# A Conformer layer: later weight loads and weight preparation, and a depthwise convolution shifted so that it no longer waits for the next group

## The chip, the cores and the metric

The kernel runs on one core of one Trainium2 chip. The metric is the device time of one execution in microseconds (us), lower is better.

Engines as the profile names them: PE is TensorE (matmuls and transposes), PEld its weight loads, DVE VectorE, ACT ScalarE, POOL GpSimd, SP SyncE, which issues most transfers ("SPq" is a transfer that it issues).

## The reference, cut to what matters

Two sequences (B = 2) of T = 4000 tokens with D = 512 features go through one Conformer layer in bfloat16.

```python
x1 = x  + 0.5 * silu(layernorm(x)  @ w_ff1_a) @ w_ff1_b          # FFN 1, 512 -> 2048 -> 512
h  = layernorm(x1);  q, k, v = h @ w_q, h @ w_k, h @ w_v
x2 = x1 + softmax(q @ k.T * scale) @ v @ w_o                     # attention over all 4000 tokens
h  = layernorm(x2) @ w_pw1;  h = h[..., :D] * sigmoid(h[..., D:])  # gate (GLU)
dc = depthwise_conv(h, dw)                                       # 15 taps along time, 7 to each side
dc = (dc - mean) / sqrt(var + 1e-5)                              # over both sequences: all of dc first
x3 = x2 + silu(dc) @ w_pw2
out = layernorm(x3 + 0.5 * silu(layernorm(x3) @ w_ff2_a) @ w_ff2_b)
```

## The kernel before

The kernel works on groups of 500 tokens: 8 groups (NG) per sequence, each of 4 tiles (TPG) of 125 tokens (P). Per sequence, phase A does FFN 1 and the projections of all groups. Phase B does attention, gate and convolution. After both sequences phase D does the rest. The weights w_q and w_k are multiplied together once at the start, and so are w_v and w_o (the "weight fusion").

The framework's scheduler fixes one static list of instructions per engine when the kernel is built. It orders them by a priority that counts up in program order, and by its own estimate of when things are ready. `tc.cur_priority` lets the program move a piece forward (a lower number) or back.

Attention of one tile takes four blocks of 1000 keys. Each block is a chain over three engines:

```python
def attention_tile(qg, x1g, x2g, i):
    for j in range(NBLK):                                    # 4 blocks
        sps = psum.tile(..., name="s_ps", tag="s")           # two buffers in all
        ...   8 matmuls: scores                              # PE   s_ps
        nc.vector.tensor_reduce(negm[:, j:j+1], sps, op=ALU.max, negate=True)   # DVE  negm
        nc.scalar.activation(pexp, sps, ACT.Exp, bias=negm[:, j:j+1], ...)      # ACT  pexp
        ...   8 transposes of pexp                           # PE   pt_ps
        nc.scalar.copy(pts, ptp)                             # ACT  pt_sb
        ...   8 matmuls with V                               # PE   o_ps
        nc.scalar.copy(obuf[:, j, :], ops)                   # ACT  obuf
    ...                                                      # DVE: weights of the blocks, x2g
```

The convolution of group g is cut into four blocks of 128 channels. Five taps of a block are matmuls with diagonal matrices on PE (`conv_ps`), ten are steps on DVE (`cacc`, the last one writes `dcg`). The DVE steps get a low priority, so that they fill gaps. A convolution needs 7 positions of its right neighbour, so group g is only scheduled when the gate of group g + 1 is done:

```python
def conv_c(g, c, dcg):
    for k in range(NPE): ...                    # 5 matmuls on PE
    saved = tc.cur_priority
    tc.cur_priority = saved + CONV_PRIO_OFFSET  # 3000: low
    for k in range(NPE, KW): ...                # 10 steps on DVE
    nc.vector.bn_stats(...)
    tc.cur_priority = saved

def glu_front(g, x2g):
    ...                                         # norm, transposes, gate
    if g > 0:
        ...                                     # POOL copies 7 positions each way
        schedule_conv(g - 1)
    if g == NG - 1:
        schedule_conv(g)

def schedule_conv(g):
    for c in range(KD):
        pending.append(lambda c=c: conv_c(g, c, dcg))
    pending.append(lambda: conv_fin(g, dcg))    # a fifth item: only one store
```

The work of gate and convolution is handed out between the attention tiles of the next group:

```python
for g in range(NG):
    ...
    for i in range(TPG):
        attention_tile(qg, x1g, x2g, i)
        for _ in range(-(-len(pending) // (TPG - i))):      # rounded up
            pending.popleft()()
    nc.sync.dma_start(tok_view(x2s, b, g), x2g[:])
    pending.appendleft(lambda g=g, x2g=x2g: glu_front(g, x2g))
while pending:
    pending.popleft()()
```

After the first tile the gate runs and adds five items. Then ceil(5/3) = 2, ceil(3/2) = 2 and 1 items follow after tiles two, three and four. So convolution blocks stand after the second and the third tile, two each, and after the fourth only the store.

## Time and profile before

The median was 2663.91 us (2661.47 to 2666.32 in four runs).

| before | |
|---|---|
| profiled span | 2659.7 us |
| PE, DVE, ACT busy | 89%, 60%, 45% |
| steady attention group (groups 3 to 6, which repeat alike) | 80.8 us |
| attention of a sequence, first to last store of x2s | 568.6 us and 571.9 us |
| tail: last store of x2s to the first load of the next phase | 75.0 us and 74.1 us |

From the page of the kernel before: the busy times, then the busy tenths of PE, the granted PE clock and the DMA share in 40 equal slices of 66 us, then the shares of the engines in the chain of work that ended last.

```profile
PE 2374.0 (89%) x12943; PEld 1383.0 (52%) x12944; DVE 1601.4 (60%) x3004; ACT 1190.7 (45%) x1866; POOL 94.1 (4%) x119
...
PE   6999989999999972699989999999997299999998
...
PEclk8999999999999995799999999999999599999999
DMA  4111110000000000211120000000002121111100
...
PE 71%; DVE 14%; ACT 9%; DMA 2%; issue 2%; SPq 1%; POOL 0%; ACTq 0%; POOLq 0%; DVEq 0%
```

PE is the bottleneck nearly everywhere, and the holes in its row (the seams) are the start, the change from sequence 1 to sequence 2, and the end of sequence 2's attention. There the clock falls as well.

The timeline of SP gives the rhythm of phase B, as one x2s store ends each group (columns: start, duration of the issue, engine, line, operation, output<-input, count).

```profile
665.27 0.27 SPq L426 DMA_DIRECT2D x2s<-x2g  x1
...
746.09 0.27 SPq L426 DMA_DIRECT2D x2s<-x2g  x1
...
987.35 0.26 SPq L426 DMA_DIRECT2D x2s<-x2g  x1
...
1062.36 0.38 SPq L109 DMA_DIRECT2D wa<-in_w_ff_a_dram  x1
...
1063.34 11.35 SPq L223 DMA_DIRECT2D xg<-in_x_dram  x2
```

A steady group takes 746.09 - 665.27 = 80.8 us. From the last group of sequence 1 (987.35) 75 us pass until the loads of sequence 2 are issued (1062.36), weights first, x behind them. The steady group as a window (columns: from and to, length, then the busy us of PE, PEld, DVE, ACT and POOL with their numbers of instructions, the PE clock, the DMA share, GB/s):

```profile
665.27:746.09 80.82, 77.66 (x456) 46.94 (x454) 67.85 (x115) 46.96 (x73) 1.83 (x3) 1.00 0.08 26
```

PE is recorded busy for 77.7 of 80.8 us; 3.2 us are idle.

### The profile page before, as it was taken

Reading aid. Unit: us, or ns where it says so; the run is one execution under the profiler, and the core shown is the slowest. Engines: PE = TensorE matmul, PEld = TensorE weight load, DVE = VectorE, ACT = ScalarE, POOL = GpSimd, SP = SyncE. Lnnn points to the kernel's source line nnn. Section 1 sums busy time; section 2 is a strip of 40 time slices with the busy share of each in tenths; the row PEclk is TensorE's granted clock in tenths of the full one; section 3 lists DMA queues with packets and bytes.
Section 4 is the critical chain, followed back from the end, with each engine's and each line's share of the span. In section 5 each row is a group of like instructions: output and inputs, shape, how many; then the busy total and the mean of one; then the engine's idle time right before and its main releaser. Section 6 shows DMA issues by size and latency. Waiting matters only on the chain.

```text
span 2659.7 us, 32574 instructions
## 1 busy us (share of the span) xinstructions
PE 2374.0 (89%) x12943; PEld 1383.0 (52%) x12944; DVE 1601.4 (60%) x3004; ACT 1190.7 (45%) x1866; POOL 94.1 (4%) x119
## 2 busy tenths in 40 slices
PE   6999989999999972699989999999997299999998
PEld 3555555555555540355545555555554055555554
DVE  3344345598888888344334558988888844444443
ACT  2433255555555540233426556555553143334432
POOL 0000000000000000000000000000000000000000
PEclk8999999999999995799999999999999599999999
DMA  4111110000000000211120000000002121111100
GB/s 119 47 46 33 47 39 24 24 32 13 20 32 32 17 16 17 97 39 43 39 70 16 16 24 32 32 14 19 32 16 87 54 63 47 47 47 47 39 25 23
DMA packets 77065, 101.32 MB, mean 38 GB/s; under 512 B 9456, under 2 KB 66160, under 8 KB 76912
## 3 DMA queue, kind: packets, MB, share of 16 engines
q1 hardware_dynamic: 76912, 99.24, 11.6%
q8 instruction: 101, 1.65, 0.3%
q14 instruction: 52, 0.43, 0.1%
HBM read 58.28 MB, written 40.96 MB: 37 GB/s over the span
## 4 chain that ended last, share of the span: by engine, by line
PE 71%; DVE 14%; ACT 9%; DMA 2%; issue 2%; SPq 1%; POOL 0%; ACTq 0%; POOLq 0%; DVEq 0%
PE ff_acc L200 17%; PE ff_ps L188 17%; PE o_ps L392 16%; PE s_ps L370 7%; DVE cacc L306 6%; ACT pt_sb L389 5%; PE pt_ps L387 3%; DVE negm L376 3%; PE q_ps L246 2%; PE pwb_ps L339 2%; PE pwa_ps L347 2%; PE pw_ps L470 2%; PE v_ps L258 2%; ACT pexp L380 2%; ACT obuf L395 1%
## 5 line engine op out<-in xcount | busy, mean ns | idle before, releaser
L370 PE MATMUL s_ps<-KT,qgB 128*125 128x500 bf16 x2048 | 506.0, 376 | 8.9 <-issue 4.6
L392 PE MATMUL o_ps<-V,pt_sb 125*125 125x512 bf16 x2048 | 486.8, 383 | 16.6 <-ACT pt_sb L389 4.5
L188 PE MATMUL ff_ps<-ln_hT,wa 128*128 128x500 bf16 x2048 | 444.2, 376 | 8.5 <-DVE ln_hT L179 8.4
L200 PE MATMUL ff_acc<-wb,ff_h 128*125 128x512 bf16 x2048 | 447.3, 379 | 0.0
L192 ACT ACTIVATE ff_h<-ff_ps 128x500 bf16<-128x500 f32 x512 | 300.3, 587 | 328.0 <-PE ff_ps L188 326.9
L376 DVE TENSOR_REDUCE negm<-s_ps 125x1 f32<-125x1000 f32 x256 | 306.0, 1196 | 207.2 <-PE s_ps L370 206.6
L380 ACT ACTIVATE pexp<-s_ps,negm 125x1000 bf16<-125x1000 f32 x256 | 280.0, 1094 | 262.3 <-DVE negm L376 184.5
L392 PEld LDWEIGHTS <-pt_sb 125*125 125x125 bf16 x2048 | 263.0, 136 | 229.4 <-ACT pt_sb L389 100.6
L200 PEld LDWEIGHTS <-ff_h 128*125 128x125 bf16 x2048 | 278.4, 137 | 160.3
L306 DVE SCALAR_TENSOR_TENSOR cacc<-gt,dwT,cacc 128x500 f32<-128x500 bf16 x512 | 355.0, 729 | 0.2
L370 PEld LDWEIGHTS <-qgB 128*125 128x125 bf16 x2048 | 260.3, 137 | 129.7 <-issue 12.8
L188 PEld LDWEIGHTS <-wa 128*128 128x128 bf16 x2048 | 199.4, 97 | 246.1 <-issue 18.1
L389 ACT COPY pt_sb<-pt_ps 125x1000 bf16<-125x1000 bf16 x256 | 251.8, 991 | 82.7 <-PE pt_ps L387 79.4
L395 ACT COPY obuf<-o_ps 125x512 f32<-125x512 f32 x256 | 149.1, 582 | 155.2 <-PE o_ps L392 155.0
L387 PEld LDWEIGHTS <-pexp 125*125 125x125 bf16 x2048 | 156.5, 137 | 116.1 <-ACT pexp L380 85.1
L387 PE MATMUL pt_ps<-ident,pexp 125*125 125x125 bf16 x2048 | 166.3, 222 | 54.6 <-ACT pexp L380 54.6
L181 ACT COPY ln_hT<-ln_tr 128x1000 bf16<-128x1000 bf16 x48 | 47.7, 993 | 323.0 <-PE ln_tr L176 323.0
L159 POOL TENSOR_TENSOR ln_rstd<-ln_ve,mhalf 125x4 f32<-125x4 f32 x80 | 86.8, 1089 | 2234.5 <-DVE ln_ve L157 2219.0
L176 PE MATMUL ln_tr<-ident,ln_hn 125*128 125x125 bf16 x1024 | 74.7, 227 | 92.3 <-DVE ln_hn L165 92.3
L473 DVE TENSOR_TENSOR x3g<-pw_ps,x2gD 125x512 bf16<-125x512 f32 x64 | 42.2, 679 | 182.2 <-PE pw_ps L470 182.2
L297 PE MATMUL conv_ps<-gt,diagw 128*128 128x500 bf16 x320 | 83.1, 403 | 44.2 <-DVE cacc L306 43.9
L176 PEld LDWEIGHTS <-ln_hn 125*128 125x128 bf16 x1024 | 65.3, 101 | 109.4 <-issue 51.7
(84 smaller groups left out, 1749.8 us busy)
## 6 DMA issues: line engine op xcount, KB each, us to landing
xg<-in_x_dram SPq DMA_DIRECT2D x16, 500.0 KB
x1s<-x1g SPq DMA_DIRECT2D x16, 500.0 KB
qts<-qg SPq DMA_DIRECT2D x16, 500.0 KB
qgB<-qts SPq DMA_DIRECT2D x16, 500.0 KB
x1gB<-x1s SPq DMA_DIRECT2D x16, 500.0 KB
x2s<-x2g SPq DMA_DIRECT2D x16, 500.0 KB
dcs<-dcg SPq DMA_DIRECT2D x16, 500.0 KB
dcgD<-dcs SPq DMA_DIRECT2D x16, 500.0 KB
```

Source lines behind the costliest of these rows:

```text
L176: nc.tensor.transpose(tr[:, kk, i, :P], hn[:, i, k * 128 : (k + 1) * 128], ident[:P, :P])
L188: nc.tensor.matmul(ps[:, :G], wa[:, k, f * 128 : (f + 1) * 128], hT[:, k, :], start=(k == 0), stop=(k == KD - 1))
L192: nc.scalar.activation(h1[:], ps[:, :G], ACT.Silu)
L200: nc.tensor.matmul(ps[:P, :D], h1s[f][:, i * P : (i + 1) * P], wb[:, f, :], start=(f == 0), stop=(f == KF - 1))
L306: nc.vector.scalar_tensor_tensor(o_ap, gt[:, c, k : k + G], dwT[:, c, k : k + 1], in1, op0=ALU.mult, op1=ALU.add)
L370: nc.tensor.matmul(sps[:P, c, :G], qg[:, k, i * P : (i + 1) * P], KT[:, k, j * KB + c * G : j * KB + (c + 1) * G], start=(k == 0), stop=(k ...
L376: nc.vector.tensor_reduce(negm[:, j : j + 1], sps[:P, :CPB, :G], axis=AX.XY, op=ALU.max, negate=True)
L380: nc.scalar.activation(pexp[:], sps[:P, :CPB, :G], ACT.Exp, bias=negm[:, j : j + 1], scale=1.0, accum_out=lsum[:, j : j + 1],)
L387: nc.tensor.transpose(ptp[:P, u, :P], pflat[:, u * P : (u + 1) * P], ident[:P, :P])
L389: nc.scalar.copy(pts[:], ptp[:P, :UPB, :P])
L392: nc.tensor.matmul(ops[:P, :D], pts[:, u, :], V[:, j * UPB + u, :], start=(u == 0), stop=(u == UPB - 1))
L395: nc.scalar.copy(obuf[:, j, :], ops[:P, :D])
```

## The change

The change wants to shorten the places where PE stands idle. It has two halves.

*Loads.* The first x tile is loaded before the FFN weights, and the first FFN weight in four chunks. The weight fusion moves behind the first half of the first FFN, its loads to ACT's queue.

*Convolution.* Output positions are shifted left by 7. The convolution of group g then needs only its own group and 14 positions of its left neighbour, and is scheduled by the gate of group g itself. One group instead of two is left after the last attention tile. Each block stores its own result, so the fifth pending item is gone.

```diff
-                wa = load_weight(wpool, w_ff1_a, "wa1")
-                wb = load_weight(wpool, w_ff1_b, "wb1")
+                wa = alloc_weight(wpool, w_ff1_a, "wa1")
+                wb = alloc_weight(wpool, w_ff1_b, "wb1")
 ...
                 xg_c, hT_c = a_front(0)
+                fill_weight(wa, w_ff1_a, col_chunks=4)
+                fill_weight(wb, w_ff1_b)
                 h1_c = ffn_a(h1pool, psum, hT_c, wa)
+                if b == 0:
+                    fused_weight_prep(wpool, psum)           # was: at the very start
 ...
-                def conv_c(g, c, dcg):
+                def conv_c(g, c, gt):
+                    o0 = PAD if g == 0 else 0
+                    o1 = G + PAD if g == NG - 1 else G
+                    W = o1 - o0
+                    pos0 = g * G - PAD + o0
 ...
+                    nc.sync.dma_start(dcs[b, :, c, pos0 : pos0 + W], dcc[:, :W])
                     tc.cur_priority = saved
-                def conv_fin(g, dcg):
-                    nc.sync.dma_start(dcs[ch], dcg[:])
 ...
-                    if g > 0:
-                        prev = gts[g - 1]
-                        nc.gpsimd.tensor_copy(gt[:, :, 0:PAD], prev[:, :, G : G + PAD])
-                        nc.gpsimd.tensor_copy(prev[:, :, PAD + G : PAD + G + PAD], gt[:, :, PAD : 2 * PAD])
-                        schedule_conv(g - 1)
-                    if g == NG - 1:
-                        schedule_conv(g)
+                    (before the gate) nc.gpsimd.tensor_copy(gt[:, :, 0:LH], prev_gt[0][:, :, G : G + LH])
+                    for c in range(KD):
+                        pending.append(lambda c=c: conv_c(g, c, gt))
```

("..." marks cuts. Phase D only follows the new layout of dcs and loads its first FFN weight in chunks.)

## The prediction

> **What bounds it now.** The page shows PE busy 2374 of 2660 us (89%); in the FFN stretches (1092 to 1359, 2150 to 2648) PE is busy over 98% at clock 1.00, so they cannot shrink. Steady attention groups (80.8 us apart by the stores of x2s) have PE busy 77.8 of 81, DVE 67.8. What is left are the seams, seen in the chain in order of time and the timeline:
> - Start: x is queued behind 6 MB of weights, first read at 31.3 us, although the weight fusion ended near 26; first FFN matmul 40.9.
> - End of attention, batch 0: last attention matmul at 983, last convolution on DVE at 1060, its store landed at 1062. DVE runs two groups' convolutions alone, 8 of one channel block each; one is 10 steps of about 0.65 us and a statistic of 0.6, 7.1 us; four are 28.4.
> - Start of batch 1: both FFN weights (4 MB) are issued at 1062.4 before x; x is read at 1080.4, first FFN matmul 1089.9.
> - Batch 1 has the same tail (2032 to 2111), then the last phase, whose weights are already there.
>
> **What the change does.**
> 1. Convolution g no longer waits for the right neighbour (output shifted 7 positions to the left), so one group instead of two is left after the last attention tile. The instruction order confirms: 40 steps of the last group plus 10 left over, against 84. In their place group 1 of each batch gets a convolution. Group 1 takes 83.1 us without any, group 2 82.6 with one, steady ones 80.8: I expect it to be free. Gain 28 us per batch, 56 in all; the 10 left-over steps fill DVE gaps (6 us) of the gate's matmuls.
> 2. Batch 1, x before weights: a 500 KB load alone landed in 3.4 us (dcgD at 2113). From there to the first FFN matmul took 9.5 us, of which 1.5 is a wait and 1.2 another tile's statistics; so 7. First FFN matmul 10.5 us after the issue instead of 27.5: gain 17. The first 512 KB chunk of weights lands sooner at the 250 GB/s of 1062 to 1080.
> 3. Start: x lands near 11 us (the tap loads ahead of it land at 9.8), the 20 diagonal builds (3.3 us) sit inside its normalization, FFN starts near 21. Then the weight fusion, some 12 us with its waits (wv and wo reuse the buffers of wq and wk, so load late); the second FFN matmul group starts near 49 instead of 56. Gain 7. Loads on the ACT queue gain little in themselves: the Trainium skill, "Trainium Kernel Development and Optimization", Key Constraints, says that queues share the same 16 DMA engines and only issue time is saved.
> 4. Added: 4 stores of 126 KB for one of 500 KB, 1000-byte rows in the last phase's loads. Both off the chain (DMA share 4 to 9% in attention).
>
> 1, 2 and 3 all lie on the chain, as PE is idle there. Sum 28+28+17+7 = 80. Prediction 2585 us, range 2562 to 2614; faster by over 2% 0.88, within 2% 0.11, slower 0.01.
>
> **What would show it.** Last attention matmul to last convolution 48 us instead of 77; x issue to FFN in batch 1 10 to 12 us; first FFN matmul at 19 to 24; attention groups still 80 to 83 us; PE busy time unchanged.
>
> **What would make it wrong.** The fourth convolution moves to the group's last tile, so its low-priority DVE steps may hold up the next group's maxima: 1 us per group costs 14. Group 1 may grow. The late wv/wo loads may stall PE at the start.

## The result, and the profile after

The changed kernel takes 2650.1 us (2645.96 to 2653.55, 9 runs), the kernel before 2662.47 us (13 runs). The ratio is 0.995, with a 95% interval of 0.9941 to 0.996: no difference by the 2% criterion, where 3% were predicted.

The same lines of the page, for the changed kernel:

```profile
PE 2377.3 (90%) x12942; PEld 1379.3 (52%) x12944; DVE 1612.6 (61%) x2998; ACT 1186.8 (45%) x1866; POOL 93.5 (4%) x105
...
PE   5999989989999994799989999999998399999998
...
PEclk9999999999999997899999999999999699999999
DMA  4110110100001000311020001000000411111100
...
PE 61%; DVE 26%; ACT 7%; issue 2%; DMA 2%; POOL 1%; SPq 0%; ACTq 0%; POOLq 0%; DVEq 0%
```

PE's work is the same (2377.3 for 2374.0 us). The holes at the ends of attention became smaller, as intended (their slices 7 2 became 9 4 in sequence 1 and 7 2 became 8 3 in sequence 2). Between the holes the slices are too coarse to show a loss, but DVE's share of the chain rose from 14% to 26%, with DVE's work up by only 11 us. The same places in the timeline of SP:

```profile
674.72 0.27 SPq L437 DMA_DIRECT2D x2s<-x2g  x1
...
759.58 0.27 SPq L437 DMA_DIRECT2D x2s<-x2g  x1
...
1014.87 0.27 SPq L437 DMA_DIRECT2D x2s<-x2g  x1
...
1062.09 0.29 SPq L236 DMA_DIRECT2D xg<-in_x_dram  x1
1062.42 6.05 SPq L116 DMA_DIRECT2D wa<-in_w_ff_a_dram  x4
```

The tail shrank from 75.0 to 1062.09 - 1014.87 = 47.2 us. But a steady group now takes 759.58 - 674.72 = 84.9 us for 80.8. In its window the work is the same to within 1.1 us on every engine:

```profile
674.72:759.58 84.86, 78.22 (x454) 46.61 (x453) 68.94 (x115) 46.65 (x73) 1.66 (x2) 1.00 0.08 25
```

PE's idle time in it is 84.86 - 78.22 = 6.6 us, for 3.2 before.

Laid out along the time axis, the two profiled spans differ by 11.2 us, which adds up so:

| stretch | predicted | measured, before minus after, us |
|---|---|---|
| start, to the first matmul of the second FFN half | 7 | 56.15 - 54.97 = 1.2 |
| attention of sequence 1 | 0 | 568.6 - 597.3 = -28.7 |
| tail of sequence 1 | 28 | 75.0 - 47.2 = 27.8 |
| sequence 2, loads issued to first FFN matmul | 17 | 27.5 - 15.5 = 12.0 |
| attention of sequence 2 | 0 | 571.9 - 595.7 = -23.8 |
| tail of sequence 2 | 28 | 74.1 - 49.7 = 24.4 |
| all else (rest of phase A, phase D) | 0 | -1.7 |
| sum | 80 | 11.2 |

The tails gave 52.2 us, and attention took 52.5 us back. That is the main question. The second is why start and second sequence gave 13 for 24.

Where does PE stand idle in a group, if the work is the same? The list of waits in the steady group (engine, line and tile that waited, what released it, then us in total, times, longest) names the transposes of the exponentials. Before:

```profile
ACT pexp L380 <- DVE negm L376: 9.8, 12, 1.5
...
PEld L387 <- ACT pexp L380: 3.2, 3, 1.7
...
PE pt_ps L387 <- ACT pexp L380: 2.1, 2, 1.3
```

After:

```profile
ACT pexp L389 <- DVE negm L385: 14.3, 11, 2.1
...
PEld L396 <- ACT pexp L389: 8.2, 7, 2.0
...
PE pt_ps L396 <- ACT pexp L389: 5.3, 4, 1.6
```

The transposes waited 5.3 us for the exponentials instead of 2.1 (their weight loads, which overlap PE, 8.2 instead of 3.2), in a group that grew by 4.0. One such place in the timeline of the changed kernel (a bracket is idle time before, and its releaser):

```profile
737.96 1.94 PE L401 MATMUL o_ps<-V,pt_sb 125*125 125x512 bf16 x8
...
739.73 2.06 PE L379 MATMUL s_ps<-KT,qgB 128*125 128x500 bf16 x9
...
740.14 0.74 DVE L421 SCALAR_TENSOR_TENSOR x2g<-obuf,cw,oacc 125x512 bf16<-125x512 f32 x1
740.80 2.29 DVE L385 TENSOR_REDUCE negm<-s_ps 125x1 f32<-125x1000 f32 x2
742.08 1.09 ACT L389 ACTIVATE pexp<-s_ps,negm 125x1000 bf16<-125x1000 f32 x1 [1.56 <-DVE negm L385]
...
743.19 1.09 ACT L389 ACTIVATE pexp<-s_ps,negm 125x1000 bf16<-125x1000 f32 x1
...
743.32 0.67 PE L396 MATMUL pt_ps<-ident,pexp 125*125 125x125 bf16 x8 [1.52 <-ACT pexp L389]
...
744.37 3.84 DVE L330 SCALAR_TENSOR_TENSOR cacc<-gt,dwT,cacc 128x500 f32<-128x500 bf16 x5
...
745.36 2.97 PE L401 MATMUL o_ps<-V,pt_sb 125*125 125x512 bf16 x13
```

PE does nine score matmuls in a row (739.73): by count and semaphores, the last one of a block and all eight of the next. What its list has next are the transposes of the first of these two blocks. Its maximum on DVE, its exponential on ACT and then its transposes follow one after the other, and PE stands 1.52 us. Part of that is DVE, which starts the maximum 0.7 us after the scores end, because it still has x2g to do; the rest is that eight matmuls are shorter than the detour. The output matmuls of an earlier block (737.96), which could have filled the gap, stand in the list before the last score matmul; those at 745.36 need these very transposes.

### The profile page after: what moved, and what is told of

It reads as the page before. It is cut to its first block, busy times and chain, and to the rows that moved or that the text cites. A ratio compares the mean times of both kernels' runs of the same rounds, so it can differ in the third digit from the quotient of the medians.

```text
span 2648.5 us, 32618 instructions
## 1 busy us (share of the span) xinstructions
PE 2377.3 (90%) x12942; PEld 1379.3 (52%) x12944; DVE 1612.6 (61%) x2998; ACT 1186.8 (45%) x1866; POOL 93.5 (4%) x105
## 4 chain that ended last, share of the span: by engine, by line
PE 61%; DVE 26%; ACT 7%; issue 2%; DMA 2%; POOL 1%; SPq 0%; ACTq 0%; POOLq 0%; DVEq 0%
PE ff_acc L213 17%; PE ff_ps L201 17%; PE o_ps L401 9%; DVE cacc L330 9%; DVE negm L385 6%; PE s_ps L379 5%; DVE oacc L421 3%; ACT pt_sb L398 3%; ACT pexp L389 3%; PE pt_ps L396 2%; PE q_ps L259 2%; PE pw_ps L487 2%; PE v_ps L271 2%; PE pwa_ps L361 1%; DVE x2g L421 1%
## 5 line engine op out<-in xcount | busy, mean ns | idle before, releaser
L330 DVE SCALAR_TENSOR_TENSOR cacc<-gt,dwT,cacc 128x500 f32<-128x500 bf16 (+2 forms) x512 | 362.7, 732 | 3.5
L398 ACT COPY pt_sb<-pt_ps 125x1000 bf16<-125x1000 bf16 x256 | 251.7, 990 | 86.5 <-PE pt_ps L396 85.0
L396 PE MATMUL pt_ps<-ident,pexp 125*125 125x125 bf16 x2048 | 167.8, 224 | 98.6 <-ACT pexp L389 97.9
L216 DVE SCALAR_TENSOR_TENSOR x1g<-ff_acc,xg 125x512 bf16<-125x512 f32 x64 | 44.0, 688 | 104.4 <-PE ff_acc L213 104.4
```

The costliest lines, as they stand in the source:

```text
L330: nc.vector.scalar_tensor_tensor(o_ap, gt[:, c, o0 + k : o0 + k + W], dwT[:, c, k : k + 1], in1, op0=ALU.mult, op1=ALU.add)
L396: nc.tensor.transpose(ptp[:P, u, :P], pflat[:, u * P : (u + 1) * P], ident[:P, :P])
L398: nc.scalar.copy(pts[:], ptp[:P, :UPB, :P])
```

## The experiments

All outputs are right. Steady group means a stretch between two neighbouring x2s stores in the middle of sequence 1.

### Is it the hand-out of the blocks? (e1, e2)

The change drops the fifth pending item. Four items over three tiles are handed out 2, 1, 1 instead of 2, 2, 1, so the fourth block moves behind the group's last tile. e1 gives the changed kernel an empty fifth item; e2 takes the fifth item from the kernel before.

```diff
 # e1, on the changed kernel
                     for c in range(KD):
                         pending.append(lambda c=c: conv_c(g, c, gt))
+                    pending.append(lambda: None)
 # e2, on the kernel before
-                    for c in range(KD):
+                    for c in range(KD - 1):
                         pending.append(lambda c=c: conv_c(g, c, dcg))
-                    pending.append(lambda: conv_fin(g, dcg))
+                    pending.append(lambda: (conv_c(g, KD - 1, dcg), conv_fin(g, dcg)))
```

> The changed kernel with one empty item put back on the pending list, after the four convolution blocks, so that the list has five items again and the rounding-up split hands out 2, 2, 1 per tile (blocks 0,1 in tile 1, blocks 2,3 in tile 2, nothing in tile 3) as in the kernel before, in place of 2, 1, 1. Nothing else differs. Theory A (the spread over the tiles cost the time, because the fourth block's steps now stand before the next group's maxima): steady attention groups go from 84.9 back to about 80.8 us, total about 2650 - 50 = 2600 us, ratio to before about 0.977. Rival B (a convolution one group earlier is not free, whatever its place in the group): groups stay at 84.9, total 2650, ratio 0.995. Rival C (the four small stores or the three-deep dcc ring hold up DVE or the queue): also stays at 84.9.

> The kernel before with its closing item (the store) folded into the fourth block's item, so that the list has four items and is handed out 2, 1, 1. Nothing of the change is in it. Theory A: its steady groups go from 80.8 to about 84.9 us in groups 2 to 7 of both batches, total about 2663 + 12 x 4 = 2710 us, ratio about 1.018. Rivals B and C: same time as before, ratio 1.00, groups 80.8.

e1 took 2603.5 us (ratio to before 0.9786, 0.9769 to 0.9802), its steady groups 80.8 us. e2 took 2706.24 us (1.0167, 1.0151 to 1.0182), its steady groups 84.9 us. So an item that does nothing gives 47 us back to the changed kernel, and the kernel before, with nothing of the change in it but four items for five, falls to the same 84.9. The hand-out is the cause. How it acts was still open.

### Four stores for one? (e3)

```diff
-                    dcc = work.tile([128, 512], BF16, name="dcc", tag="dcc", bufs=3)
+                    dcc = dcg[:, c, :]                 # one tile for the four blocks of a group
-                    nc.sync.dma_start(dcs[b, :, c, pos0 : pos0 + W], dcc[:, :W])
+                    if c == KD - 1:
+                        nc.sync.dma_start(dcs[b, :, :, pos0 : pos0 + W], dcg[:, :, 0:W])
```

> The changed kernel with one 500 KB store per group, issued after the fourth block, from a two-deep tile as in before, in place of four stores of 126 KB from a three-deep ring; still four items, 2, 1, 1. Theory A: no change, steady groups 84.9, total 2650 within 5 us. Rival C: groups back to about 81, total about 2600.

It took 2650.37 us with groups of 84.9. The stores cost nothing, and that rival falls.

### Why x came late in sequence 2 (e4)

In the changed kernel x stands first in the queue, yet DVE reads it 8.6 us after its issue (1070.70 - 1062.09, below), where the prediction took 3.4 us from another 500 KB load. One difference is that x is laid over 125 partitions, the other (dcgD) over 128 (dcgD also comes in longer rows; e4 tests the partitions). The Trainium skill, "DMA: Bandwidth & Descriptors", section "Why a DMA increments its semaphore by 16 and not by 1", says that a transfer runs on the largest number of engines up to 16 that divides the size of the slowest dimension on both its sides; by that rule 125 gives 5, 120 gives 15. e4 loads the first x tile of each sequence as 120 + 5 partitions.

```diff
-                    nc.sync.dma_start(xg[:], tok_view(x, b, g))
+                    if g == 0:
+                        xv = tok_view(x, b, g)
+                        nc.sync.dma_start(xg[0:120], xv[0:120])
+                        nc.sync.dma_start(xg[120:P], xv[120:P])
+                    else:
+                        nc.sync.dma_start(xg[:], tok_view(x, b, g))
```

> The changed kernel with the first x tile of each batch loaded as 120 + 5 partitions in place of 125. In the profile of after the first x tile of batch 1 took 8.5 us from issue to first use though nothing was queued ahead of it, with a DMA share of 0.31, that is 5 of 16 engines; 125 has the divisor 5 and 120 the divisor 15. Theory D (few engines carry the tile): issue to first use about 4 us, first FFN matmul of batch 1 about 11 us after the issue instead of 15.5, total 4 to 8 us below the changed kernel. Rival E (the weights issued behind x take its bandwidth): issue to first use stays at 8 us, total unchanged.

The windows just after the issue in sequence 2 (the last two columns are the mean DMA share of 16 engines and GB/s, the column before them the PE clock), first of the changed kernel, then of e4:

```profile
1062.00:1066.00 4.00, 0.00 (x0) 0.00 (x0) 0.00 (x0) 0.00 (x0) 0.00 (x0) 0.50 0.31 89
```

```profile
1056.30:1060.90 4.60, 0.00 (x0) 0.00 (x0) 0.00 (x0) 0.00 (x0) 0.00 (x0) 0.50 0.80 186
```

A share of 0.31 is 5 of 16 engines, and 89 GB/s over 4 us are 356 KB, less than the 512 KB of x, although the weights were being issued behind it from 1062.42 on. With the split the share is 0.80 (the weights behind x included, as 186 GB/s over 4.6 us are more than x). DVE reads x 4.6 us after its issue instead of 8.6. The first reads of x on DVE, first in the changed kernel (issue at 1062.09), then in e4 (issue at 1056.30):

```profile
1070.70 1.29 DVE L167 BATCH_NORM_STATS2 ln_st<-xg 125x6 f32<-125x512 bf16 x2 [9.81 <-DMA wa<-in_w_ff_a_dram]
```

```profile
1060.93 1.29 DVE L167 BATCH_NORM_STATS2 ln_st<-xg 125x6 f32<-125x512 bf16 x2 [5.76 <-DMA xg<-in_x_dram]
```

e4 took 2640.96 us (0.9922, 0.9907 to 0.9937), 9 us less than the changed kernel (5.0 of them before the first x2s store, 2.3 between the sequences). The page and the trace agree. (The first line names wa as the releaser, which this instruction does not read; the profile infers releasers from semaphore events.)

### Which part of the hand-out matters? (e5, e6)

A block behind the last tile may cost by its place. Or, what the timeline suggests, maxima that stand next to each other in DVE's list may cost. e5 hands out 2, 1, 1, 1 and e6 1, 0, 2, 2, both on the changed kernel.

```diff
-                        for _ in range(-(-len(pending) // (TPG - i))):
+                        for _ in range(min(len(pending), (2, 1, 1, 1)[i])):     # e6: (1, 0, 2, 2)
```

> The changed kernel with a fixed hand-out: gate and block 0 after tile 0, then one block after each of tiles 1, 2 and 3. Block 3 is again handed out after the group's last tile, as in the changed kernel. Theory A1 (it is the block after the last tile that costs): groups near 84.9 or worse, total 2645 to 2660 us. Theory A2 (it is how the static DVE order bunches: in the changed kernel a steady group has four places where two maxima stand directly one after the other, twice with a run of 7 or 8 convolution steps beside them; the fast order has two, both in the gate's tile; this order has none, runs of at most 5): groups at 80.8 or less, total 2580 to 2605 us.

> The changed kernel with blocks 0 and 1 after tile 2 and blocks 2 and 3 after tile 3, so that even more of the convolution stands in the next group. Theory A1: groups longer than 84.9, total 2650 us or more. Theory A2: this order has one adjacent pair of maxima per steady group and runs of at most 7: groups about 81, total 2595 to 2620 us.

The edit of e5 does not do quite what its expectation says. In the first group with a convolution only the gate waits when the loop asks for two items, so block 3 is left over each time: in a steady group block 3 of the convolution before stands behind the first tile, and blocks 0, 1, 2 behind the others. There is still one block behind each tile, but five blocks are left after the last group instead of four. So compare the groups and not the totals here: from the last attention matmul to the last convolution step e5 takes 54.8 and 55.5 us and e6 51.9 and 53.5, the changed kernel 46.7 and 49.2.

e5 took 2632.02 us with groups of 82.8 us, e6 2609.85 us with groups of 81.3 to 81.5 us. e6 has two blocks behind the last tile and its groups are nearly the fastest, so the place by itself is not it. e5 has no neighbouring maxima in its list and still lies in the middle, so the count of neighbouring maxima is not it either. Both readings failed.

### The loading half alone, and the taps behind the weights (e7, e8)

e7 is the kernel before with only the loading half. e8 is the changed kernel with the loads of the taps, and the 20 diagonal matrices built from them, moved behind the FFN weights.

```diff
 # e7, on the kernel before
+                fill_weight(wa, w_ff1_a, col_chunks=4)       # and the rest of the loading half
 # e8, on the changed kernel
-    for c in range(KD):
-        nc.sync.dma_start(dw_bf[:, c, :], dw[...].rearrange("k p -> p k"))    # at the very start
                 if b == 0:
                     fused_weight_prep(wpool, psum)
+                    tap_prep()                               # the same loads and builds here
```

> The kernel before with only the loading half of the change: x ahead of the weights, first FFN weight in column chunks, weight fusion after the first FFN half; convolution, halo and stores as before. If the halves add up, this one gains what the seams show: about 1 us at the start and 12 at the start of batch 1, total about 2650 us, ratio 0.995, with groups at 80.8; the convolution half then gives 0 in the changed kernel (gain of about 52 at the tails, loss of about 52 in the groups).

> The changed kernel with the four loads of the depthwise taps (2-byte pieces) and the 20 diagonal builds moved behind the FFN weights. In after the queue issues x only at 8.5 us, behind the taps, and the builds (3.3 us) stand inside the first normalization. If that is what made the start late: x issued near 1 us, first FFN matmul near 13 to 16 instead of 29 (the first weight chunk may now be what it waits for), the second FFN half 10 to 13 us earlier, total about 2638 us. If the start is bound by the bytes instead (x and the first chunk behind other loads), first FFN matmul stays above 22.

e7 took 2651.64 us (0.9955, 0.994 to 0.9969): the loading half alone is worth what the whole change is worth, and the convolution half nets nothing.

e8 took 2647.81 us, 2.3 less than the changed kernel, which is within the spread of the runs of the two. What holds x at the start is visible in the queue of the changed kernel:

```profile
0.74 7.72 SPq L90 DMA_DIRECT2D dw_bf<-in_dw_dram  x4
8.50 1.76 SPq L236 DMA_DIRECT2D xg<-in_x_dram  x1
```

The issue of four tap loads, element by element, occupies the queue until 8.5 us, and x needs 10.6 us more. Two things share these: the packets of the taps, which move until 12.7 us (DVE's first read of them), and the few engines of x, as split it needs only 6.9 us (e4: issued at 8.17, read at 15.08). In e8 x is first, and the first FFN matmul starts at 19.5 us for 29.1, but the second half of the FFN starts at 53.3 for 55.0. The tap loads now held the queue from 12.8 to 27 us, the second x tile landed at 35.2, and DVE, with its list in order, reached the copies for the weight fusion only after it. The delay had moved behind the first half.

### A maximum's priority (e9)

e9 keeps everything of the changed kernel and only raises the priority of the maxima.

```diff
+                        saved = tc.cur_priority
+                        tc.cur_priority = saved - 200
                         nc.vector.tensor_reduce(negm[:, j : j + 1], ...)
+                        tc.cur_priority = saved
```

> The changed kernel; hand-out of blocks stays 2, 1, 1 after the tiles, nothing else of the work changed; only the maxima of attention get a higher scheduling priority (200 steps earlier), so the scheduler puts them in other places of VectorE's instruction list (steady group: two neighbouring pairs of maxima instead of four) and TensorE's list loses the spot where two blocks of output matmuls stand together around a convolution. Theory A (the static order that the hand-out leads to costs the 4 us per group, not the place of the blocks itself): steady groups 80.8 to 82, total 2600 to 2612, waits of the transposes for pexp near 3 us per group instead of 8. Rival R (blocks of convolution after the third and the last tile cost in themselves, whatever the order of the maxima): groups 84 to 85, total 2640 to 2650.

It took 2624.37 us (0.9858, 0.9844 to 0.9873), with groups of 83.2 us: neither what one reading said nor what the other did. But it showed that 26 us hang on order alone, with the same blocks behind the same tiles.

### A third reading: how much work PE has between a block's scores and its transposes

PE's list was then compared instead of DVE's. A block is from here on one of the four key blocks of an attention tile, 16 in a group. Between the last score matmul of a block and its first transpose, maximum and exponential must run, which take 1.2 and 1.1 us. PE can only fill that time with what its list has in between. The Trainium skill, "PSUM — Partial Sum Buffer", section "Engine vs sequencer instructions", says that matmuls start and complete in program order and that the queues of the other engines are strict FIFO. No run here tests whether a ready matmul would overtake: the output matmuls behind the stall at 743.32 needed its transposes.

Two cuts from the lists of a steady group, as "output tile * number of instructions". The first is the usual pattern, which occurs in both kernels. The second is one of the bad places of the changed kernel:

```
s_ps*5 o_ps*8 s_ps*3 pt_ps*8        three last scores of a block, two of the next, outputs of the block before, three more scores of the next, then the transposes
o_ps*8 s_ps*9 pt_ps*8 s_ps*3 pt_ps*8 s_ps*2 o_ps*16      outputs first; then one last score, eight of the next block, the transposes at once
```

In each list the work between was added up for each of the 16 blocks of a group, with about 0.2 us for a matmul and 0.08 us for a transpose (an estimate from the durations in the trace), and the blocks with less than 1.8 us were counted. The threshold was chosen after seven kernels had been seen, so e12 to e15 were the test.

| kernel | short blocks in a steady group | transposes' weight loads wait for pexp, us | steady group, us |
|---|---|---|---|
| before | 2 | 3.2 | 80.8 |
| e1 empty item | 2 | 3.2 | 80.8 |
| e6 hand-out 1,0,2,2 | 2 | 4.6 | 81.3 to 81.5 |
| e5 hand-out 2,1,1,1 | 3 | 4.9 | 82.8 |
| e9 maxima first | 3 | 5.3 | 83.2 |
| after | 6 | 8.2 | 84.9 |
| e3 one store | 6 | 8.2 | 84.9 |
| e2 before, four items | 6 | 8.5 | 84.9 |

Group 1 of each sequence has 6 to 8 short blocks in every kernel so far (7 in the kernel before). It took 83.1 us in the kernel before although it has no convolution at all there.

### The test: the same edit where it should hurt, and an order without short blocks (e12, e13, e15)

e12 is e1 with the edit of e9. There the edit raises the count in a steady group from 2 to 6 (group 2 has 5, group 3 only 3). e13 is the changed kernel with the scores and the maxima raised by 50 steps, which leaves no short block. e15 is the kernel before with the same edit as e13.

```diff
 # e13, on the changed kernel; e15: the same on the kernel before
                         sps = psum.tile([128, 2, 512], FP32, name="s_ps", tag="s")
+                        saved = tc.cur_priority
+                        tc.cur_priority = saved - 50
                         ...                                  # 8 score matmuls
                         nc.vector.tensor_reduce(negm[:, j : j + 1], ...)
+                        tc.cur_priority = saved
```

> The kernel of e1 (fast hand-out 2, 2, 1 with the empty fifth item) with the maxima raised by 200 steps as in e9. The same change that helped the changed kernel is expected to hurt here. A count in the two instruction lists, made before the run: blocks of scores in a steady group for which TensorE's list holds under 1.8 us of other matmuls between the block's last score matmul and its first transpose: before 2, after 6, e1 2, e2 6, e5 3, e6 2, e9 3; here 6. Theory B (this look-ahead on TensorE sets the group's time: 2 gave 80.8 to 81.4 us, 3 gave 82.8 to 83.2, 6 gave 84.9): groups 84 to 86 us, total 2640 to 2670, slower than e1 by 40 to 60 us. Theory A (neighbouring maxima on VectorE; here 3 pairs, between 2 and 4): 82 to 83 us. Rival R (the place of the blocks, which is that of e1): 80.8 us.

> The changed kernel, hand-out 2, 1, 1 as it is, with the score matmuls and the maxima raised by 50 steps: in TensorE's list no block is left with under 1.8 us between its scores and its transposes (count 0; it was 6), and no two maxima are neighbours on VectorE. Theory B: steady groups at or below 80.8, 78.5 to 80.8 (TensorE is busy 78.2 us of one), total 2570 to 2610. Rival R: 84 to 85, 2640 to 2650. If the scores run so far ahead that the next stage, the buffers of the exponentials, fills up, groups may be above 81; then the count alone doesn't set the time.

> The kernel before, nothing of the change in it, with the score matmuls and the maxima raised by 50 steps as in e13; count of blocks with under 1.8 us of look-ahead 0 (it was 2). Theory B: steady groups 77.5 to 78.5 as in e13. Attention of a batch took 568.6 us there from the first to the last store of x2s, and 543 in e13: minus 24 per batch, total 2605 to 2625. Then, with the order of attention made alike in both kernels, the change itself is worth 65 to 85 us (against 2540 of e13), the sum that was predicted for tails, batch 1 and start. If before stays near 2655, the gain of e13 is bound to the changed convolution and not to the order.

e12 took 2652.6 us, 49 us more than e1; four groups took 83.9 to 86.9 us, and groups 2 and 3, with the odd counts, 89.9 and 78.6. The edit that saved 26 us in the changed kernel cost 49 here, as the count said, and against both older readings. (Group 3 alone does not fit the count; together the two groups took 168.5 us.)

e13 took 2539.84 us (0.9538, 0.9524 to 0.9553), 110 us less than the changed kernel, by order alone, and below the expected 2570 to 2610. Its steady groups take 78.1 us, a little less than expected. In the window of one, the waits of the transposes for pexp are gone altogether; what remains around them is the wait of the output matmuls' weight loads for the copied transposes, and of that copy for the transposes:

```profile
PEld L404 <- ACT pt_sb L401: 5.2, 12, 0.8
...
ACT pt_sb L401 <- PE pt_ps L399: 3.4, 2, 2.4
```

```profile
649.61:727.72 78.11, 76.97 (x454) 47.72 (x452) 67.35 (x115) 45.93 (x73) 1.24 (x2) 1.00 0.09 27
```

PE is recorded busy for 77.0 of 78.1 us. The total fell by more than the steady groups alone account for, because the bad groups gained most: group 1 went from 89.2 to 77.5 us and group 7 from 85.5 to 75.4.

e15 took 2599.47 us (0.9758, 0.9742 to 0.9775) with groups of 77.7 us. With the order alike in both kernels, the change is worth 2599.47 - 2539.84 = 60 us. The two traces give the parts: 0.3 at the start, 40.9 between the last x2s store of sequence 1 and the first of sequence 2, 27.4 after the last one, and 8.1 lost inside attention, 3 of them in each group 1, which has a convolution now and had none (77.5 for 74.6 us). Expected were 65 to 85 for the change and 2605 to 2625 for e15, so the saving was there all along, and a little smaller than thought.

The pages give the idle time over all 256 blocks. The columns are the busy time of the transposes, the mean ns of one, then the idle time of PE just before them and what ended it; first the kernel before, then the changed one, e13 and e15.

```profile
L387 PE MATMUL pt_ps<-ident,pexp 125*125 125x125 bf16 x2048 | 166.3, 222 | 54.6 <-ACT pexp L380 54.6
```

```profile
L396 PE MATMUL pt_ps<-ident,pexp 125*125 125x125 bf16 x2048 | 167.8, 224 | 98.6 <-ACT pexp L389 97.9
```

```profile
L399 PE MATMUL pt_ps<-ident,pexp 125*125 125x125 bf16 x2048 | 234.0, 220 | 0.0
```

```profile
L390 PE MATMUL pt_ps<-ident,pexp 125*125 125x125 bf16 x2048 | 233.0, 220 | 0.0
```

So the changed kernel has 44 us more of idle time before the transposes, most of the 52.5 us that attention lost, and in e13 and e15 there is none. A rival is that DVE comes late to the maxima. Added up from the traces at the stalls, it began them 34.5 us late in the changed kernel and 12.8 in the kernel before, so up to half of the growth came that way; 20 and 6 us of it went to convolution steps and statistics. But over all blocks the maxima begin later in e13 (86.5 us in sum) than in the changed kernel (73.5), and PE does not stand once. Enough work in PE's list hides both the detour and DVE's delay.

### Together (e10, e11, e14)

e10 joins to e1: x tiles split 120 + 5 for the first two groups, the taps as one contiguous load of 15 rows turned on PE, the four weights of the fusion on SP behind the FFN weights with buffers of their own, and more buffers for the loads of phase D (dcgD four, x2gD three, for two), of which the first two x2 tiles are split too. e11 also gives all 15 taps of the last group of a sequence to PE. e14 is e11 with the edit of e13.

```diff
 # e10 (main parts)
+    dw_raw = wp.tile([KW, D], BF16, name="dw_raw")
+    nc.sync.dma_start(dw_raw[:], dw[:, :])                   # then 4 transposes on PE
-        wv_sb = load_weight(wp, w_v, "wv_sb", eng=nc.scalar, tag="prep_a")
+        wv_sb = load_weight(wp, w_v, "wv_sb", tag="prep_e")
 # e11
+                    npe = KW if g == NG - 1 else NPE
+                    for k in range(npe): ...                 # matmuls
+                    if npe == KW:
+                        nc.scalar.copy(dcc[:, :W], pc[:, :W])
```

> What was learnt, together: the empty fifth item (fast order), the first two x tiles of each batch loaded as 120 + 5 partitions, the taps loaded with one contiguous load of 15 rows and turned on TensorE in the weight fusion instead of element by element in front of x, wq wk wv wo behind the FFN weights on one queue with own buffers, one more buffer for the two loads of the last phase and its first two x2 tiles split too. From 2603.5: x split 9, start 5 to 8 more, seam before the last phase about 9. If these gains add: 2575 to 2585. If the start is bound by the arrival of 6 MB of weights and not by the order: 2590 to 2596. Steady groups 80.8 as before.

> As e10, and in the last group of each batch all 15 taps are done by TensorE (15 matmuls per block) instead of 5 there and 10 steps of 0.65 us on VectorE: if the tail is bound by VectorE's 40 steps (28 us), it becomes 60 matmuls of about 0.21 us, or 0.42 at half clock, of which 20 were there: gain 12 to 20 us per batch, 24 to 40 in all under e10. If the tail is bound by the gate's chain and not by the convolution, under 10 in all. The ten further diagonals per block are built in group 0, 40 builds of about 0.16 us on VectorE: group 0 at most 7 us longer.

> e11 (2550.7) with the score matmuls and the maxima raised by 50 steps. Its steady groups are 80.8 with a count of 2; here 0. Theory B: groups 78.5 to 80.3, 14 groups, total 2515 to 2545. If nothing is left to gain beyond a count of 2: 2545 to 2555.

e10 took 2582.73 us, inside the range, though not for the parts expected. The start gave 15.7 us (to the first x2s store, 401.4 for 417.1), more than thought; the start of sequence 2 gave 2.4, the seam before phase D 2.1 where 9 were expected. The second half of the first FFN now starts at 39.5 us instead of 55.0:

```profile
12.64 14.88 PE L205 MATMUL ff_ps<-ln_hT,wa 128*128 128x500 bf16 x64
...
39.52 3.19 PE L217 MATMUL ff_acc<-wb,ff_h 128*125 128x512 bf16 x14
```

e11 took 2550.69 us, 32 less, 15.5 and 14.5 in the two tails: the tail was bound by DVE's steps. e14 took 2485.85 us (0.9334, 0.9319 to 0.935), with groups of 77.5 us, again below what was expected (2515 to 2545). It beats both kernels, by 178 us over the one before in its own rounds.

## Why the prediction was wrong, point by point

**Tails, 28 + 28: right.** They gave 27.8 and 24.4 us. From the last attention matmul to the last convolution step the traces have 46.7 and 49.2 us for 76.4 and 78.7, where 48 for 77 were predicted.

**"Group 1 of each batch gets a convolution. ... I expect it to be free", and "attention groups still 80 to 83 us": wrong, and this is the step that failed.** Attention lost 28.7 and 23.8 us. The prediction saw that the fourth block moves to the last tile and named it as what could make it wrong, with "1 us per group costs 14"; but it gave a result within 2% only 11% and looked for the harm in low-priority DVE steps in front of the maxima. Convolution work on DVE did delay maxima at the stalls, by 20 us in all for 6 before, a third of the growth at most. What the runs show is that the hand-out (e1, e2) changes the order of PE's own list, and that the count of blocks with too little work between scores and transposes goes with the time of a group (e12, e13 and e15, foretold with it in direction; e13 and e15 gained more than was foretold). PE stood 98.6 us before the transposes instead of 54.6. The cost was not in the amount of work that was moved, nor in its place by itself (e6), but for the most part in where attention's own instructions then stood. The premise was wrong too: the 83.1 us of group 1 without any convolution was read as room for one. It was a group with 7 short blocks. In an order without them it took 74.6 us, and a convolution added 3.

**Sequence 2, 17: too large, 12 measured.** The term mis-sized is the x load: 3.4 us were taken from a 128-partition tile, the 125-partition tile needed 8.6 us (e4: 4.6 when split); these 5 us are what was missing. The mechanism was right.

**Start, 7: 1.2 measured.** "x lands near 11 us" failed: it was read at 19.1, issued at 8.5 behind the taps; few engines account for part of that (6.9 us when split in e4, for 10.6). The first FFN matmul came at 29.1 instead of 21, and the fusion after the first FFN half took the estimated 12 us (11.2). Putting the taps later alone did not mend it (e8); loading them contiguously, together with the split of x and the new place of the fusion's loads, did (e10).

**Stores off the chain: right** (e3; the shorter rows of phase D's loads were not tested by themselves). **Work unchanged: right**, PE 2377.3 for 2374.0 us. The point from the Trainium skill, "Trainium Kernel Development and Optimization", Key Constraints, on queues that share 16 DMA engines was not tested by itself; no run here moves loads between queues alone.

**Still open:** what inside the scheduler turns 2, 1, 1 into that list was not followed, nor why e9 and e5, both with three short blocks, differ by 0.4 us. The count is a coarse measure: the groups of e6 have 2 and take 0.5 to 0.7 us more than before. And some 8 of the 52.5 us that attention lost are not idle time before the transposes.

## What to carry to other kernels

When an engine's list is fixed in advance, a change that only moves low-priority filler can reorder the critical work around it, so after such a change read the new list: between a producer and its consumer on the bottleneck engine there must be as much other work as the detour over the other engines takes. Raise the priority of what starts that detour (here scores and maxima), and do this before judging any other change, since it was worth about 64 us in one kernel and 110 in the other and hid a real saving of 60. When a load's time is taken from another load, compare the partitions as well as the bytes.

## What the Trainium skill lacked or had wrong

- "DMA: Bandwidth & Descriptors", "Why a DMA increments its semaphore by 16 and not by 1": the rule for the number of engines holds here (share 0.31, 5 of 16, for a 125-partition tile). The page's "Rules for kernel authors" advise against two transfers to disjoint partition halves, as both run on all 16 engines anyway, and for one 128-partition transfer; the exception is not named that a 125-partition tile gains from a split into 120 + 5, 4.6 us for 8.6 from issue to first use.
- The same page has no figure for the issue of an element-wise rearranged load: four loads of 128 x 15 two-byte elements occupied the queue for 7.7 us in the changed kernel, and 14.3 us in e8 when larger loads were queued ahead.
- "Perfetto Trace Analysis", "Optimization Strategy": it says that gaps that repeat on the engine that should be saturated can mean too few buffers. Here they came from the order of the list: with no buffer changed, a steady group went from 84.9 to 78.1 us (e13).
- "PSUM — Partial Sum Buffer", "Engine vs sequencer instructions": nothing here contradicts execution in order, and nothing tests it. No page that bears on this draws the consequence for a static schedule, how much other work must stand between a block's scores and its transposes; here under 1.8 us in 2, 3 and 6 of 16 blocks went with 80.8 to 81.5, 82.8 to 83.2 and 84.9 us in the kernels of the table.
- "TensorE: Matmul & The Clock Gate", "Part 1: The HAM clock gate": nothing wrong; a clock at half rate after idle time agrees with the seams, where PE had no matmul and the granted clock was 0.50 (1062 to 1066 us).
